# Retention attention and a two-layer feed-forward in one TensorE stream, token group by token group

## The chip, the cores and the metric

The kernel runs on one core of one Trainium2 chip. The metric is device time in microseconds (us) of one execution, median of several runs. A profile is one execution recorded by the hardware profiler; its span runs from the first to the last instruction.

Engines in the profile: PE is TensorE (matmuls), PEld its weight loads, DVE is VectorE, ACT is ScalarE, POOL is GpSimd (here it also issues the loads that convert to bf16), SP is SyncE. The kernel before has runs of about 303 to 307 us span and runs of about 310 to 311 us; the latter are marked slow. Ratios below use fast runs only.

## The reference, cut to what matters

```python
def _attn_ref(q, k, v):                       # q, k, v: (4, 8, 768, 64) float32
    gamma = 1.0 - 2.0 ** (-5.0 - np.arange(H))
    for t in range(S):
        state = gamma * state + outer(k[t], v[t])      # per batch and head: 64 x 64
        y[t] = (1 / sqrt(64)) * (q[t] @ state)

def _moe_ref(x, w_in, w_out, alpha):          # x: (3072, 512), 512 -> 2048 -> 512
    h = x @ w_in
    s = np.sin(alpha * h)
    g = h + s * s / (alpha + 1e-09)
    return g @ w_out
```

A chunked form of the attention works on 128 tokens at a time: within a chunk, a masked 128x128 score matrix; from earlier chunks, the state. There are 4 batches x 6 chunks = 24 chunks, 8 heads each.

## The kernel before

It has two stages, one after the other. Attention, per chunk index c and batch b (cuts marked `# ...`):

```python
for c in range(n_chunks):
    nc.gpsimd.dma_start(out=q_c, in_=dram_chunk(q, c))     # also k_c, v_c: 512 KB each
    nc.vector.tensor_mul(kw_c, k_c, wj_bc)                 # decay of k
    nc.scalar.copy(shat_bf[:64], shat_f32)                 # state to bf16
    for b in range(B):
        for h in range(H):                                 # q scaled and transposed
            nc.tensor.matmul(ptq[:64, h, :], q_c[:, b, h, :], Sgi[:, h, :], ...)
        nc.scalar.copy(qdT_gi, ptq[:64])
        # ... the same for k: 8 transposes, one ScalarE copy to kdT
        for h in range(H):                                 # scores, 64 rows of the array
            nc.tensor.matmul(psA[:, h, :], kdT[:, h, :], qdT_gi[:, h, :], ...)
        nc.vector.tensor_mul(aT, psA, mask01_bc)
        # ... psY: 8 matmuls with the state, 8 with v; ScalarE scales it into y_sbuf
        # ... psS: 8 matmuls k x v
        nc.vector.tensor_add(shat_f32[:, b], shat_f32[:, b], psS[:64])
    nc.vector.tensor_mul(shat_f32, shat_f32, gC_bc)        # decay of the state
```

Then the weights, and the feed-forward in 6 groups of 512 tokens:

```python
for g in range(n_groups):
    # ... 16 transposes of y_sbuf and 4 VectorE copies make xT (features on partitions)
    for ff in range(FF_SUB):                               # 16 steps
        for ks in range(K_SUB):                            # 4 matmuls of 512 columns
            nc.tensor.matmul(psH, w_in_bf[:, ks, ff, :], xT[:, ks, :], ...)
        nc.scalar.activation(out=s_sb, in_=psH, func=SIN, scale=alpha_sb[:, ff:ff + 1])
        nc.scalar.activation(out=s_sb, in_=s_sb, func=SQR, scale=rsq_alpha[:, ff:ff + 1])
        nc.vector.tensor_add(g_bf, psH, s_sb)
        for ts in range(n_tok_sub):                        # 4 matmuls of 512 columns
            nc.tensor.matmul(psO[ts], g_bf[:, ts * 128:(ts + 1) * 128], w_out_bf[:, ff, :], ...)
```

Of the kernel before, what the change touches and what calls it, by code (L numbers as in the profile page):

```python
# [9 lines left out]
F32 = mybir.dt.float32  # L10
BF16 = mybir.dt.bfloat16
EXP = mybir.ActivationFunctionType.Exp
SIN = mybir.ActivationFunctionType.Sin
SQR = mybir.ActivationFunctionType.Square
CPY = mybir.ActivationFunctionType.Copy
SQRT = mybir.ActivationFunctionType.Sqrt
# [3 lines left out]
def kernel(  # L20
# [13 lines left out]
    n_chunks = S // C  # L34
    BH = B * H
    NT = BH * n_chunks
    assert S % C == 0 and D == 64 and C == 128

    d_model = H * D
    d_ff = moe_w_in.shape[1]  # L40
    n_tok = B * S
    K_SUB = d_model // 128
    FF_SUB = d_ff // 128
    scale = 1.0 / math.sqrt(D)

    gammas = [1.0 - 2.0 ** (-5.0 - h) for h in range(H)]
# [3 lines left out]
    work = ctx.enter_context(tc.tile_pool(name="work", bufs=2))  # L50

    ident = consts.tile([128, 128], BF16, name="ident")
    make_identity(nc, ident)

    iota_free = consts.tile([128, 128], F32, name="iota_free")
    nc.gpsimd.iota(iota_free, pattern=[[1, 128]], channel_multiplier=0, base=0,
                   allow_small_or_imprecise_dtypes=True)
    iota_p = consts.tile([128, 1], F32, name="iota_p")
    nc.gpsimd.iota(iota_p, pattern=[[0, 1]], channel_multiplier=1, base=0,
                   allow_small_or_imprecise_dtypes=True)  # L60

    gi_free = consts.tile([128, H, 128], F32, name="gi_free")
    Sgi = consts.tile([128, H, 128], BF16, name="Sgi")
    wj_all = consts.tile([128, H], F32, name="wj_all")
    gC_all = consts.tile([128, H], F32, name="gC_all")
    for h in range(H):
        lng = math.log(gammas[h])
        nc.scalar.activation(out=gi_free[:, h, :], in_=iota_free, func=EXP, scale=lng)
        nc.vector.tensor_mul(Sgi[:, h, :], ident, gi_free[:, h, :])
        nc.scalar.activation(out=wj_all[:, h:h + 1], in_=iota_p, func=EXP, scale=-lng)  # L70
        nc.gpsimd.memset(gC_all[:, h:h + 1], gammas[h] ** C)
# [3 lines left out]
                            compare_op=mybir.AluOpType.is_ge, fill=0.0,  # L75
                            channel_multiplier=-1, base=0)
    mask01_bc = mask01[:, None, :].to_broadcast([128, H, 128])

    shat_f32 = big.tile([64, B, H, D], F32, name="shat_f32")
    nc.gpsimd.memset(shat_f32, 0.0)  # L80

    y_sbuf = big.tile([128, n_chunks, B, H, D], BF16, name="y_sbuf")

    gi_bc1 = gi_free[:64, :, :]
    gC_bc = gC_all[:64, None, :, None].to_broadcast([64, B, H, D])
    wj_bc = wj_all[:, None, :, None].to_broadcast([128, B, H, D])

    def dram_chunk(t, c):
        return t[:, :, c * C:(c + 1) * C, :].rearrange("b h s d -> s b h d")

    with tc.tile_pool(name="psum_r", bufs=1, space=bass.MemoryType.PSUM) as psr:
        for c in range(n_chunks):
            q_c = work.tile([128, B, H, D], BF16, name="q_c", tag="q_c", bufs=3)
            kw_c = work.tile([128, B, H, D], BF16, name="kw_c", tag="kw_c", bufs=3)
            v_c = work.tile([128, B, H, D], BF16, name="v_c", tag="v_c", bufs=3)
            k_c = work.tile([128, B, H, D], BF16, name="k_c", tag="k_c", bufs=3)
            nc.gpsimd.dma_start(out=q_c, in_=dram_chunk(q, c))  # L97
            nc.gpsimd.dma_start(out=k_c, in_=dram_chunk(k, c))  # L98
            nc.gpsimd.dma_start(out=v_c, in_=dram_chunk(v, c))  # L99
            nc.vector.tensor_mul(kw_c, k_c, wj_bc)  # L100

            shat_bf = work.tile([64, B, H, D], BF16, name="shat_bf", tag="sh")
            nc.scalar.copy(shat_bf[:64], shat_f32)  # L103

            for b in range(B):
                ptq = psr.tile([64, H, 128], F32, name="ptq", tag="qtg", bufs=1)
                for h in range(H):
                    nc.tensor.matmul(ptq[:64, h, :], q_c[:, b, h, :], Sgi[:, h, :],  # L108
                                     start=True, stop=True)
                qdT_gi = work.tile([64, H, C], BF16, name="qdT_gi", tag="qdT_gi")  # L110
                nc.scalar.copy(qdT_gi, ptq[:64])  # L111

                ptk = psr.tile([64, H, 128], BF16, name="ptk", tag="pt", bufs=2)
                for h in range(H):
                    nc.tensor.transpose(ptk[:64, h, :], kw_c[:, b, h, :], ident)  # L115
                kdT = work.tile([64, H, C], BF16, name="kdT", tag="kdT")
                nc.scalar.copy(kdT, ptk[:64])  # L117

                psA = psr.tile([128, H, 128], F32, name="psA", tag="psA", bufs=1)
                for h in range(H):  # L120
                    nc.tensor.matmul(psA[:, h, :], kdT[:, h, :], qdT_gi[:, h, :],  # L121
                                     start=(h % 4 == 0), stop=True, skip_group_check=True)
                aT = work.tile([128, H, 128], BF16, name="aT", tag="aT")
                nc.vector.tensor_mul(aT, psA, mask01_bc)  # L124

                psY = psr.tile([128, H, D], F32, name="psY", tag="psY", bufs=1)
                for h in range(H):
                    nc.tensor.matmul(psY[:, h, :], qdT_gi[:, h, :], shat_bf[:, b, h, :],  # L128
                                     start=(h == 0), stop=True, skip_group_check=True)
                for h in range(H):  # L130
                    nc.tensor.matmul(psY[:, h, :], aT[:, h, :], v_c[:, b, h, :],  # L131
                                     start=False, stop=True, skip_group_check=True)
                nc.scalar.mul(y_sbuf[:, c, b, :, :], psY, scale)  # L133

                psS = psr.tile([64, H, D], F32, name="psS", tag="psS", bufs=1)
                for h in range(H):
                    nc.tensor.matmul(psS[:64, h, :], kw_c[:, b, h, :], v_c[:, b, h, :],  # L137
                                     start=(h == 0), stop=True, skip_group_check=True)
                nc.vector.tensor_add(shat_f32[:, b, :, :], shat_f32[:, b, :, :], psS[:64])  # L139

            nc.vector.tensor_mul(shat_f32, shat_f32, gC_bc)  # L141

    w_in_bf = big.tile([128, K_SUB, FF_SUB, 128], BF16, name="w_in_bf")
    nc.gpsimd.dma_start(out=w_in_bf, in_=moe_w_in.rearrange("(ko ki) (fo fi) -> ki ko fo fi", ki=128, fi=128))

    w_out_bf = big.tile([128, FF_SUB, d_model], BF16, name="w_out_bf")
    nc.gpsimd.dma_start(out=w_out_bf, in_=moe_w_out.rearrange("(fo fi) n -> fi fo n", fi=128))

    alpha_sb = consts.tile([128, FF_SUB], F32, name="alpha_sb")
    for ff in range(FF_SUB):  # L150
        nc.sync.dma_start(out=alpha_sb[:, ff], in_=moe_alpha[ff * 128:(ff + 1) * 128])
    rsq_alpha = consts.tile([128, FF_SUB], F32, name="rsq_alpha")
    nc.gpsimd.tensor_scalar_add(rsq_alpha, alpha_sb, 1e-9)
    nc.scalar.activation(out=rsq_alpha, in_=rsq_alpha, func=SQRT)
    nc.vector.reciprocal(rsq_alpha, rsq_alpha)

    TOK_G = 512
    n_groups = n_tok // TOK_G
    n_tok_sub = TOK_G // 128

    out_view = out.rearrange("(t p) n -> p t n", p=128)

    with tc.tile_pool(name="psum_m", bufs=1, space=bass.MemoryType.PSUM) as psm:
        for g in range(n_groups):
            bc_list = [divmod(g * n_tok_sub + cc, n_chunks) for cc in range(n_tok_sub)]
            xT = work.tile([128, K_SUB, TOK_G], BF16, name="xT", tag="xT")
            for ks in range(K_SUB):
                pt = psm.tile([128, n_tok_sub, 128], BF16, name="ptxt", tag="psH", bufs=4)
                for cc in range(n_tok_sub):
                    b, c = bc_list[cc]  # L170
                    lhsT = y_sbuf[:, c, b, 2 * ks:2 * ks + 2, :].rearrange("p h e -> p (h e)")
                    nc.tensor.transpose(pt[:, cc, :], lhsT, ident)
                nc.vector.tensor_copy(xT[:, ks, :], pt.rearrange("p c s -> p (c s)"))  # L173

            psO = [psm.tile([128, d_model], F32, name=f"psO{ts}", tag=f"psO{ts}")
                   for ts in range(n_tok_sub)]
            for ff in range(FF_SUB):
                psH = psm.tile([128, TOK_G], F32, name="psH", tag="psH", bufs=4)
# [46 lines left out]
```

## Time and profile before

| | |
|---|---|
| median, all runs of the first series | 307.45 us (306.78 to 312.24, 4 runs) |
| profiled span (state slow by its clock, see below) | 310.9 us |
| wait for the first load | 0 to 13 us |
| attention | 13 to 114 us |
| feed-forward | 114 to 311 us, 31.0 us per full group |

First the profile page of the kernel before: the span in 40 equal slices, each digit a busy share in tenths, with the granted clock of TensorE and the GB/s that the loads moved.

```profile
span 310.9 us, 4916 instructions
...
PE   0189697969899977999899989998999899989991
...
PEclk9999979965955557999999999999999999999997
DMA  2999999999990000000300030003000300030003
GB/s 11 133 151 147 147 145 147 148 148 191 209 194 4 0 2 0 0 2 0 135 1 2 0 135 2 1 0 137 0 0 0 138 0 0 0 137 0 0 1 135
```

Loads fill the first 93 us. In the trace's clock records TensorE ran at half clock from 65 to 79 us and from 86 to 120 us. These records begin with the first change, at 24.2 us here. Before it the row reads 9 without a measurement: matmuls of 128 columns start 107 ns apart there, and 56 ns apart at full clock. How much of the attention runs at half clock differs from run to run: the profiled run has a mean clock of 0.912, like the runs marked slow (0.906 to 0.918), while the fast ones have 0.925 to 0.956.

Next, the busy time of each engine in one full group of the feed-forward, from one group's first output copy to the next group's (columns: the stretch, its length, busy us and count of each engine, then clock, DMA share, GB/s).

```profile
core 0: us, PE busy (x) PEld busy (x) DVE busy (x) ACT busy (x) POOL busy (x), PEclk, DMA share, GB/s
210.34:241.33 30.99, 29.64 (x142) 12.68 (x144) 14.62 (x24) 20.17 (x32) 0.00 (x0) 1.00 0.09 34
```

A group takes 31.0 us in this trace (five periods of 30.99 us), not the 32.0 us that the prediction and the expectation of e2 assume. TensorE looks 96% busy (29.64 of 30.99). That is not how full it is: a matmul's record (0.38 us for 512 columns) is longer than its distance to the next. Eight back to back take 1.90 us; their starts are 0.216 us apart, so the group's 128 matmuls need 27.6 us. The Trainium skill says this in "Trainium Kernel Development and Optimization", section "Performance Expectations": matmul busy time is a bad metric of distance to the peak. The trace agrees; the experiment e2 below takes 2.5 us out of such a "96% busy" group. With 0.9 us for the group's 16 transposes (56 ns each), 2.5 us of the 31.0 are waiting.

What the rest waits for is in the list of waits (engine and line, what it waited for, total us, times, longest):

```profile
DVE g_bf L186 <- ACT s_sb L184: 96.6, 66, 5.0
ACT s_sb L183 <- PE psH L180: 59.6, 23, 4.2
PEld L188 <- DVE g_bf L186: 30.4, 61, 1.9
PE psO L188 <- DVE g_bf L186: 5.2, 9, 1.4
```

The second layer's weight load (PEld L188: here g_bf is the stationary operand) waits for the sum that VectorE makes, which waits for sine and square on ScalarE.

### The profile page before, as it was taken

To read this page: it belongs to the slowest core of one execution; us is meant where nothing else is said; L and a number is where in the kernel's file an instruction comes from. 1 tells how busy PE (TensorE), PEld (TensorE's weight loads), DVE (VectorE), ACT (ScalarE), POOL (GpSimd) and SP (SyncE) were. 2 spreads that over 40 slices of the span, in tenths; PEclk is the share of its full clock that TensorE was granted. 3 is DMA by queue.
4 is the path that set the end of the run, shared out by engine and by line. 5 is a ranking of instruction groups with operands and counts; after the bars stand their busy time and mean duration, and the time that the engine had idled before them with its cause. 6 is when DMAs were issued, how large, how long until landed. Compare 5 with 4: busy or idle time off the path is not lost.

```text
span 310.9 us, 4916 instructions
## 1 busy us (share of the span) xinstructions
PE 264.5 (85%) x1999; PEld 150.8 (49%) x2016; DVE 160.5 (52%) x213; ACT 198.0 (64%) x290; POOL 35.9 (12%) x40
## 2 busy tenths in 40 slices
PE   0189697969899977999899989998999899989991
PEld 0177586758687763444443444444444444444430
DVE  2047879687756472434643464346434643463433
ACT  7147869765976626676567656765666566656660
POOL 9444444550000000000000000000000000000000
PEclk9999979965955557999999999999999999999997
DMA  2999999999990000000300030003000300030003
GB/s 11 133 151 147 147 145 147 148 148 191 209 194 4 0 2 0 0 2 0 135 1 2 0 135 2 1 0 137 0 0 0 138 0 0 0 137 0 0 1 135
DMA packets 82389, 20.23 MB, mean 65 GB/s; under 512 B 76736, under 2 KB 78784, under 8 KB 82368
## 3 DMA queue, kind: packets, MB, share of 16 engines
q0 software_dynamic: 76608, 13.63, 89.7%
q1 hardware_dynamic: 5760, 6.30, 5.9%
q8 instruction: 15, 0.25, 0.4%
q14 instruction: 6, 0.05, 0.1%
HBM read 27.27 MB, written 6.29 MB: 108 GB/s over the span
## 4 chain that ended last, share of the span: by engine, by line
PE 44%; ACT 16%; issue 13%; DVE 12%; POOL 8%; DMA 5%; ACTq 0%; POOLq 0%; DVEq 0%
PE psO L188 25%; PE psH L180 9%; ACT s_sb L183 8%; ACT s_sb L184 6%; DVE g_bf L186 5%; DMA k_c<-in_k_dram 3%; PE psA L121 3%; POOL q_c L97 3%; DVE o_sb L193 2%; POOL k_c L98 2%; POOL v_c L99 2%; DVE aT L124 2%; PE ptq L108 2%; PE ptk L115 2%; DVE shat_f L141 1%
## 5 line engine op out<-in xcount | busy, mean ns | idle before, releaser
L186 DVE TENSOR_TENSOR g_bf<-psH,s_sb 128x512 bf16<-128x512 f32 x96 | 63.9, 691 | 96.6 <-ACT s_sb L184 96.6
L183 ACT ACTIVATE s_sb<-psH,alpha_sb 128x512 f32<-128x512 f32 x96 | 62.3, 681 | 59.6 <-PE psH L180 59.6
L188 PE MATMUL psO<-w_out_bf,g_bf 128*128 128x512 bf16 x374 | 92.9, 381 | 7.6 <-DVE g_bf L186 5.2
L180 PE MATMUL psH<-xT,w_in_bf 128*128 128x512 bf16 x377 | 94.3, 384 | 2.1 <-DVE xT L173 1.4
L184 ACT ACTIVATE s_sb<-s_sb,rsq_alpha 128x512 f32<-128x512 f32 x96 | 65.8, 719 | 1.2
L188 PEld LDWEIGHTS <-g_bf 128*128 128x128 bf16 x384 | 32.2, 98 | 60.8 <-DVE g_bf L186 30.4
L180 PEld LDWEIGHTS <-w_in_bf 128*128 128x128 bf16 x384 | 37.8, 99 | 47.7 <-issue 5.4
L124 DVE TENSOR_TENSOR aT<-psA,mask 128x1024 bf16<-128x1024 f32 x24 | 29.3, 1219 | 18.2 <-PE psA L121 18.2
L111 ACT CAST qdT_gi<-ptq 64x1024 bf16<-64x1024 f32 x24 | 24.1, 1003 | 20.6 <-PE ptq L108 19.9
L108 PE MATMUL ptq<-Sgi,q_c 128*64 128x128 bf16 x192 | 21.6, 266 | 18.3 <-DMA q_c<-in_q_dram 13.0
L117 ACT COPY kdT<-ptk 64x1024 bf16<-64x1024 bf16 x24 | 24.0, 1005 | 8.2 <-PE ptk L115 4.5
L108 PEld LDWEIGHTS <-q_c 128*64 128x64 bf16 x192 | 16.4, 140 | 18.8 <-DMA q_c<-in_q_dram 13.0
L100 DVE TENSOR_TENSOR kw_c<-k_c,wj_all 128x2048 bf16<-128x2048 bf16 x6 | 13.7, 2287 | 14.8 <-DMA k_c<-in_k_dram 14.8
L115 PE MATMUL ptk<-ident,kw_c 128*64 128x128 bf16 x192 | 20.3, 263 | 1.0 <-ACT kdT L117 0.5
L121 PE MATMUL psA<-qdT_gi,kdT 64*128 64x128 bf16 x192 | 18.8, 254 | 2.7 <-DVE aT L124 2.0
L139 DVE TENSOR_TENSOR shat_f<-shat_f,psS 64x512 f32<-64x512 f32 x24 | 16.1, 673 | 7.2 <-PE psS L137 6.7
L193 DVE COPY o_sb<-psO 128x512 f32<-128x512 f32 x24 | 15.7, 689 | 7.5 <-DMA out_dram<-o_sb 4.6
L133 ACT ACTIVATE y_sbuf<-psY 128x512 bf16<-128x512 f32 x24 | 14.3, 595 | 7.5 <-PE psY L131 7.2
L115 PEld LDWEIGHTS <-kw_c 128*64 128x64 bf16 x192 | 16.5, 139 | 3.1 <-DVE kw_c L100 1.7
L121 PEld LDWEIGHTS <-kdT 64*128 64x128 bf16 x192 | 14.4, 111 | 4.6 <-issue 2.9
L128 PE MATMUL psY<-shat_bf,qdT_gi 64*128 64x64 bf16 x192 | 12.1, 214 | 4.0 <-ACT shat_bf L103 2.5
L137 PE MATMUL psS<-v_c,kw_c 128*64 128x64 bf16 x192 | 14.0, 223 | 0.4 <-DVE shat_f L139 0.4
(35 smaller groups left out, 138.9 us busy)
## 6 DMA issues: line engine op xcount, KB each, us to landing
out_dram<-o_sb SPq DMA_DIRECT2D x24, 256.0 KB, 2.1
q_c<-in_q_dram POOLq DMA_DIRECT2D x6, 512.0 KB, 10.6
k_c<-in_k_dram POOLq DMA_DIRECT2D x6, 512.0 KB, 10.5
v_c<-in_v_dram POOLq DMA_DIRECT2D x6, 512.0 KB, 10.6
w_in_bf<-in_moe_w_in_dram POOLq DMA_DIRECT2D x1, 2048.0 KB, 17.3
w_out_bf<-in_moe_w_out_dram POOLq DMA_DIRECT2D x1, 2048.0 KB, 26.6
alpha_sb<-in_moe_alpha_dram SPq DMA_DIRECT2D x16, 0.5 KB, 2.1
```

The lines of the kernel that those rows point to most:

```text
L108: nc.tensor.matmul(ptq[:64, h, :], q_c[:, b, h, :], Sgi[:, h, :], start=True, stop=True)
L111: nc.scalar.copy(qdT_gi, ptq[:64])
L115: nc.tensor.transpose(ptk[:64, h, :], kw_c[:, b, h, :], ident)
L117: nc.scalar.copy(kdT, ptk[:64])
L121: nc.tensor.matmul(psA[:, h, :], kdT[:, h, :], qdT_gi[:, h, :], start=(h % 4 == 0), stop=True, skip_group_check=True)
L124: nc.vector.tensor_mul(aT, psA, mask01_bc)
L180: nc.tensor.matmul(psH, w_in_bf[:, ks, ff, :], xT[:, ks, :], start=(ks == 0), stop=(ks == K_SUB - 1))
L183: nc.scalar.activation(out=s_sb, in_=psH, func=SIN, scale=alpha_sb[:, ff:ff + 1])
L184: nc.scalar.activation(out=s_sb, in_=s_sb, func=SQR, scale=rsq_alpha[:, ff:ff + 1])
L186: nc.vector.tensor_add(g_bf, psH, s_sb)
L188: nc.tensor.matmul(psO[ts], g_bf[:, ts * 128:(ts + 1) * 128], w_out_bf[:, ff, :], start=(ff == 0), stop=(ff == FF_SUB - 1))
L193: nc.vector.tensor_copy(o_sb, psO[ts])
```

## The change

Intent: keep TensorE fed all the time. While it runs the first layer of group g and the second layer of group g-1, it also runs, step by step, the attention of the chunks of group g+1. The new kernel walks the chunks in batch order (the six chunks of one batch in sequence), with groups of 2, 4, 4, 4, 4, 4, 2 chunks. The decay factors are put on q and k by one multiplication each, so that the state is a plain sum, which TensorE accumulates in one PSUM buffer (PSUM is the memory that the matmuls write to) over the six chunks of a batch. Two heads share one transpose (128 columns of features). The attention output comes out transposed, so it needs no transposes before the feed-forward.

The diff, cut to its core (the removed stages are those shown above):

```diff
+    groups = [2, 4, 4, 4, 4, 4, 2]
+    ctx.enter_context(tc.manual_schedule())
     ... constants: decay factors qg, kg by position and head; masks
+    def stage_scale(j, eng):                      # chunk j: q and k times their decay
+        eng.tensor_mul(qs, raw["q", j], qg[:, c, :, None].to_broadcast([128, H, D]))
+        eng.tensor_mul(ks, raw["k", j], kg[:, c, :, None].to_broadcast([128, H, D]))
+    def stage_T(j):                               # 8 transposes, one copy
+        for i, t in enumerate((st["qs", j], st["ks", j])):
+            for p in range(NP):
+                nc.tensor.transpose(pt[:, i * NP + p, :], t[:, 2 * p:2 * p + 2, :]..., ident)
+        nc.vector.tensor_copy(qkT, pt)
+    def stage_A(j):                               # scores: heads on array rows 0-63 and 64-127
+        for p in range(NP):
+            for e in range(2):
+                r = slice(64 * e, 64 * e + 64)
+                nc.tensor.matmul(pa[:, e, p, :], qkT[r, NP + p, :], qkT[r, p, :], ...)
+        nc.vector.tensor_mul(aT, pa, mask_bc)
+    def stage_Y(j):                               # output, transposed
+        if c > 0:
+            for p in range(NP):
+                nc.tensor.matmul(py[:, p, :], s_bd[c % 2][:, p, :], st["qkT", j][:, p, :], ...)
+        for p in range(NP):
+            for e in range(2):
+                nc.tensor.matmul(py[64 * e:64 * e + 64, p, :], raw["v", j][:, 2 * p + e, :],
+                                 st["aT", j][:, e, p, :], ...)
+        nc.scalar.copy(xT[g][:, :, o:o + C], py)
+    def stage_S(j):                               # state summed in PSUM
+        for p in range(NP):
+            nc.tensor.matmul(ps[:, p, :], ks pair p, v pair p, start=(c == 0 and p == 0), ...)
+        for e in range(2):
+            nc.scalar.copy(t[r, :, r], ps[r, :, r])
     ...
+    loads = w_in 0-3, chunks 2 3, w_out 0 1, chunks 4 5, w_out 2 3, chunks 6 ...
+    for fn in loads[:10]:                         # the rest: one per stage_T below
+        fn()
+    for j in range(groups[0]):
+        for fn in stages:
+            fn(j)
+    for g in range(NG + 1):
+        att = [(j, s) for the chunks j of group g+1, for s in range(4)]
+        for i in range(FF):                       # one step
+            ph = ff_in(g, i); s = ff_act(g, i, ph)         # 4 matmuls; sine, square
+            for j, sidx in att[na * i // FF:na * (i + 1) // FF]:
+                if sidx == 0:
+                    if loads: loads.pop(0)()
+                    stage_scale(j + 1, nc.vector if j + 1 < 6 else nc.gpsimd)
+                stages[sidx](j)
+            ff_add(g, i, ph, s)
+            ff_out(g - 1, i * n, n)               # n = 4 (2) second-layer matmuls
```

## The prediction

> **What bounds the kernel now.** Three stages, by the stretch table and the timeline of the trace (span 310.9 us).
>
> 1. 0 to 13 us: TensorE waits for the first q load.
> 2. 13 to 114 us: attention. The loads run at about 147 GB/s until 72 us; then the weights, 4.2 MB, until 93 us at about 205 GB/s. TensorE works in short bursts between copies; the granted clock falls to 0.5 between 64 and 116 us.
> 3. 114 to 311 us: feed-forward, 32.0 us per group of 512 tokens at clock 1.00. One layer step takes 2.0 us, though its 8 matmuls of 512 columns come 216 ns apart when back to back (8 in 1.90 us): 1.73 us. The rest is output transposes (57 ns each, 16 per group) and waits for the chain sine, square, add (0.69+0.72+0.69 us).
>
> The trace's 216 and 57 ns agree with the Trainium skill, "TensorE: Matmul & The Clock Gate", section "Back-to-back issue gap": N/2.4 GHz plus 2.5 ns.
>
> **What changes.** Per 128-token chunk TensorE now does 8 transposes, 8 score, 12 output and 4 state matmuls of 128 columns: 32 x 56 ns = 1.8 us, 41 us in all (estimate from the trace's spacing). The feed-forward stays 768 x 216 ns = 166 us. Sum: 207 us in one stream. Removed: 96 output transposes with VectorE copies (24 x 0.41 us), the state's additions, scalings and casts (16.1+13.7+11.4 us); weights load early.
>
> Per step in the steady groups: TensorE 0.86+0.45+0.86 = 2.2 us; ScalarE 1.35 + a quarter of (0.6 + two state copies of about 0.4) = 1.7 us; VectorE 0.69 + a quarter of (0.7+1.22+0.69) = 1.35 us. TensorE binds, and the sine-square-add latency (2.1 us) fits inside two steps. GpSimd scales q and k from chunk 6 on: the skill's "GPSIMD Engine Reference", section 3.1, gives 4497 ns for 2048 elements of a two-input operation; no trace here has it; my estimate is 1.3 us for 512. With three load issues of about 0.9 us (fitted to 0.76, 1.17, 1.68 us for 512, 2048, 4096 packets) that is 5.3 us per chunk, under the chunk's 7 to 9 us.
>
> **Sum (estimates).** First two chunks, serially at a cold clock: 22 us. Group 0 is paced by loads (w_in, chunks 2 to 5, w_out: about 150 to 205 GB/s) and ScalarE: ends near 47 us. Group 1 (TensorE and ScalarE both about 1.8 us per step): 30. Groups 2 to 4: 36 each, 108. Group 5: 32. Group 6 (256 tokens): 21.5. Last output matmuls 7, last copy and store 3.5. Span 249; times are about 3 us below the profiled span: **246 us**, range 236 to 262. Chances: faster by over 2% 0.97, within 2% 0.02, slower 0.01.
>
> **What would show it.** Granted clock 1.0 from about 45 us on, no 0.5 stretch after; TensorE steps of about 2.2 us with little idle; ScalarE near 75 to 80% busy there; no added activation table loads (copies run under the sine table); before that, waits named for loads, scalings, copies.
>
> **What would make it wrong.** GpSimd multiplications much slower than 1.3 us, so that scaling paces the chunks; the in-order TensorE queue stalling at attention stages behind VectorE or ScalarE; small matmuls costing more than 56 ns between the large ones; table reloads between copy and sine (1.28 us each); the start, where loads and serial stages could cost 10 us more or less.

## The result and the profile after

The new kernel took 248.03 us (247.86 to 248.22, 4 runs), the kernel before 307.45 us. The ratio of fast runs is 0.8083, with a 95% interval of 0.8033 to 0.8133. (A ratio is the mean time of one kernel's fast runs over that of the other's in the same rounds, so it is not quite the ratio of the two medians.)

The profile page of the new kernel, same rows as before:

```profile
span 246.4 us, 4059 instructions
...
PE   0146748799999999999999999999999999999993
...
PEclk9999986999999999999999999999999999999999
DMA  9999999999998879849957965901101110012112
GB/s 53 117 205 177 193 164 194 118 95 78 88 133 55 92 85 67 87 66 72 99 67 85 64 80 73 80 26 45 43 0 47 43 43 22 23 43 85 45 43 85
```

From the ninth slice on (49 us), TensorE is at 9 up to the last slice and the clock is at 9. The loads are now spread over the first 160 us.

The same trace in stretches cut at the starts of the groups (0 to 21.69: the first two chunks, where the clock of 1.00 is not measured, as said above; then groups 0, 1, 2 to 4, 5, 6; the last second layer; the last store):

```profile
0.00:21.69 21.69, 6.33 (x60) 4.41 (x61) 7.11 (x20) 5.11 (x10) 16.62 (x28) 1.00 1.26 136
21.69:51.03 29.34, 20.69 (x188) 14.68 (x188) 18.27 (x31) 20.44 (x44) 19.66 (x23) 0.88 1.85 163
51.03:79.89 28.86, 28.27 (x221) 14.22 (x222) 18.04 (x25) 25.80 (x43) 25.88 (x28) 1.00 1.25 88
79.89:183.40 103.51, 103.51 (x754) 52.11 (x753) 60.89 (x84) 80.05 (x130) 46.30 (x49) 1.00 0.65 67
183.40:214.19 30.79, 30.79 (x188) 14.80 (x187) 16.72 (x24) 24.36 (x38) 0.00 (x0) 1.00 0.10 35
214.19:235.42 21.23, 21.14 (x130) 12.62 (x129) 9.35 (x20) 16.17 (x34) 0.00 (x0) 1.00 0.13 50
235.42:242.35 6.93, 6.90 (x32) 2.94 (x30) 1.72 (x3) 0.18 (x1) 0.00 (x0) 1.00 0.20 76
242.35:246.40 4.05, 0.00 (x0) 0.00 (x0) 0.69 (x1) 0.00 (x0) 0.00 (x0) 1.00 0.17 65
```

In groups 2 to 4 TensorE has no gap (103.51 of 103.51 us); ScalarE is busy 80.05 us, 77%. Three groups take 34.5 us each and include 12 chunks of attention. The kernel before took 31.0 us for such a group without any attention.

The timeline of TensorE over some three steps in group 2 (start, length, line, what, count):

```profile
97.90 0.39 PE L134 MATMUL pt<-ident,qs 128*128 128x128 bf16 x4
98.12 0.39 PE L134 MATMUL pt<-ident,ks 128*128 128x128 bf16 x4
98.34 1.03 PE L218 MATMUL po<-w_out,gT 128*128 128x512 bf16 x4
99.21 1.03 PE L195 MATMUL ph<-xT,w_in 128*128 128x512 bf16 x4
100.17 0.40 PE L145 MATMUL pa<-qkT 64*128 64x128 bf16 x8
100.50 1.04 PE L218 MATMUL po<-w_out,gT 128*128 128x512 bf16 x4
101.37 1.03 PE L195 MATMUL ph<-xT,w_in 128*128 128x512 bf16 x4
102.33 0.41 PE L163 MATMUL py<-aT,vr 128*64 128x128 bf16 x8
102.67 1.04 PE L218 MATMUL po<-w_out,gT 128*128 128x512 bf16 x4
103.55 1.03 PE L195 MATMUL ph<-xT,w_in 128*128 128x512 bf16 x4
104.41 0.39 PE L176 MATMUL ps<-vr,ks 128*128 128x128 bf16 x4
```

From one ph to the next is one step: 2.16 us at 99.21, 2.18 us at 101.37. An attention stage fills 0.2 to 0.66 us between the two layers and none of these lines has a wait behind it.

### The profile page after: what moved, and what is told of

It reads as the page before. It is cut to its first block, busy times and chain, and to the rows that moved or that the text cites. A ratio compares the mean times of both kernels' runs of the same rounds, so it can differ in the third digit from the quotient of the medians.

```text
span 246.4 us, 4059 instructions
## 1 busy us (share of the span) xinstructions
PE 217.6 (88%) x1568; PEld 115.8 (47%) x1568; DVE 132.8 (54%) x208; ACT 172.1 (70%) x294; POOL 108.5 (44%) x127
## 4 chain that ended last, share of the span: by engine, by line
PE 72%; DMA 12%; ACT 5%; POOL 5%; issue 2%; DVE 2%; POOLq 0%
PE po L218 33%; PE ph L195 29%; DMA w_out<-in_moe_w_out_dram 5%; DMA w_in<-in_moe_w_in_dram 4%; DMA vr<-in_v_dram 3%; PE pt L134 3%; PE py L163 3%; ACT s L202 3%; PE pa L145 2%; ACT s L203 2%; PE py L159 1%; POOL qr L66 1%; PE ps L176 1%; POOL kr L66 1%; DVE gT L207 1%
## 5 line engine op out<-in xcount | busy, mean ns | idle before, releaser
L207 DVE TENSOR_TENSOR gT<-ph,s 128x512 bf16<-128x512 f32 (+1 forms) x112 | 68.7, 613 | 83.5 <-ACT s L203 83.5
L195 PE MATMUL ph<-xT,w_in 128*128 128x512 bf16 (+1 forms) x448 | 104.6, 358 | 2.1 <-DVE gT L207 1.8
L202 ACT ACTIVATE s<-ph,alpha_sb 128x512 f32<-128x512 f32 (+1 forms) x112 | 70.0, 625 | 42.9 <-PE ph L195 30.8
L218 PE MATMUL po<-w_out,gT 128*128 128x512 bf16 x384 | 98.9, 380 | 0.0
L203 ACT ACTIVATE s<-s,rsq_alpha 128x512 f32<-128x512 f32 (+1 forms) x112 | 74.0, 661 | 3.6
L195 PEld LDWEIGHTS <-w_in 128*128 128x128 bf16 x448 | 44.3, 101 | 47.4 <-issue 4.4
L218 PEld LDWEIGHTS <-gT 128*128 128x128 bf16 x384 | 33.2, 98 | 29.1
L148 DVE TENSOR_TENSOR aT<-pa,mask 128x1024 bf16<-128x1024 f32 x24 | 29.3, 1221 | 4.6 <-PE pa L145 4.6
L66 POOL DMA_DIRECT2D qr<-in_q_dram x24 | 22.5, 938 | 1.3 <-POOLq L280 0.8
L66 POOL DMA_DIRECT2D vr<-in_v_dram x24 | 21.7, 905 | 0.8 <-DMA w_in<-in_moe_w_in_dram 0.8
L66 POOL DMA_DIRECT2D kr<-in_k_dram x24 | 21.6, 899 | 0.0
L222 DVE COPY o_sb<-po 128x512 f32<-128x512 f32 x24 | 16.4, 681 | 5.0 <-PE po L218 5.0
L136 DVE COPY qkT<-pt 128x1024 bf16<-128x1024 bf16 x24 | 16.4, 682 | 2.5 <-PE pt L134 2.4
```

The lines of the kernel that those rows point to most:

```text
L66: nc.gpsimd.dma_start(out=t, in_=src[b, :, c * C:(c + 1) * C, :].rearrange("h s d -> s h d"))
L148: nc.vector.tensor_mul(aT.rearrange("p e n t -> p (e n) t"), pa.rearrange("p e n t -> p (e n) t"), mask_bc)
L195: nc.tensor.matmul(ph, w_in[:, i, f * 128:(f + 1) * 128], xT[g][:, i, :], start=(i == 0), stop=(i == KS - 1))
L202: nc.scalar.activation(out=s, in_=ph, func=ACTF.Sin, scale=alpha_sb[:, f:f + 1])
L203: nc.scalar.activation(out=s, in_=s, func=ACTF.Square, scale=rsq_alpha[:, f:f + 1])
L207: nc.vector.tensor_add(gT[g][:, f, :], ph, s)
```

## The experiments

Two questions were open after this. Where do the 59 us come from: running the attention inside the feed-forward, a leaner attention, or a feed-forward that no longer waits within its step? And what bounds the new kernel, in the middle and in its first 51 us? Below, fast runs of the variants are compared with the new kernel's 248.03 us; unedited on another chip it took 247.99 us (e0_again), so the choice of chip matters little.

### e1_seq: the new attention first, then the new feed-forward

```diff
     stage_scale(0, nc.vector); stage_scale(1, nc.vector)
     ... chunks 0 and 1 as before
+    for j in range(groups[0], NJ):
+        if loads: loads.pop(0)()
+        ... stage_scale(j + 1, nc.vector)
+        for fn in stages: fn(j)
     for g in range(NG + 1):
-        att = [(j, s) for the chunks of group g+1 ...]
+        att = []
```

> The new kernel with the attention of all 24 chunks run before the first feed-forward group (its scalings on VectorE, so that GpSimd only issues loads), everything else kept. Theory O (the gain comes mostly from running the attention inside the feed-forward): attention takes about 4 to 5 us per chunk when its stages run serially, the feed-forward about 170 to 180 us, so about 280 us (268 to 295). Rival L (the gain comes mostly from the leaner attention and the feed-forward that no longer waits within a step): at most 262 us.

Measured: 332.64 us (2 runs, ratio 1.0878 to before). It is slower than the kernel before, and slower than the range given. One chunk takes 5.03 us, as the timeline of TensorE shows:

```profile
99.67 0.58 PE L134 MATMUL pt<-ident,qs 128*128 128x128 bf16 x4
100.05 0.63 PE L134 MATMUL pt<-ident,ks 128*128 128x128 bf16 x4
101.47 0.61 PE L145 MATMUL pa<-qkT 64*128 64x128 bf16 x8 [0.79 <-DVE qkT L136]
102.01 0.61 PE L159 MATMUL py<-qkT,s_bd 128*128 128x128 bf16 x4
103.39 0.64 PE L163 MATMUL py<-aT,vr 128*64 128x128 bf16 x8 [0.78 <-DVE aT L148]
```

Every stage waits for the copy of the one before, because nothing stands between them. The transposes also run at half speed: 4 take 0.58 to 0.63 us here and 0.39 us in the new kernel, and their single starts are 107 ns apart here and 56 ns there. The feed-forward behind it took from 138.6 to 331.4 us, 193 us, not the 170 to 180 us assumed. Its first group (256 tokens, no second layer to run beside it) took 21.5 us of that, from 139.2 to 160.8 us: matmuls of 256 columns were still 213 ns apart (109 ns in the new kernel), and every two steps (2.58 us) TensorE waited 0.66 us for VectorE's sum.

### e12_seq_skew: the same, with the chunks' stages skewed

```diff
-        for fn in stages: fn(j)
+        stage_T(j)
+        if j - 1 >= groups[0]: stage_A(j - 1)
+        if j - 2 >= groups[0]: stage_Y(j - 2); stage_S(j - 2)
```

(with a few more buffers, and py in the PSUM buffers of ph.)

> As e1_seq (attention of all chunks before the feed-forward, which took 332.6 us, 5.03 us per chunk), but with the stages of neighbouring chunks skewed: transposes of chunk j, scores of j-1, output and state of j-2. If e1_seq was slow only because one chunk's stages ran as a chain with nothing between them, a chunk falls to what VectorE needs (0.68+1.22+2x0.69 = 3.3 us) or a half-clock TensorE (about 3.6 us): 24 x 1.4 us less, about 300 us (292 to 308), near the kernel before. If instead loads (2.65 us per chunk) or something else held it: 320 us or more.

Measured: 295.79 us (2 runs, ratio to before 0.9623, 0.9567 to 0.9678), inside the forecast. A chunk now takes 2.93 us and VectorE is the limit, busy in 25.00 of 25.00 us:

```profile
60.00:85.00 25.00, 16.44 (x264) 12.42 (x261) 25.00 (x35) 10.29 (x25) 24.66 (x29) 1.00 2.43 155
```

So the leaner attention together with the reordered feed-forward, but one after the other, is worth 4% over the kernel before. The remaining 48 us (295.8 to 248.0) are the difference to running them at the same time. That is a difference between two builds, not the least that overlap is worth: e12 has all scalings on VectorE, its limit, and its first feed-forward group ran at half clock (102 to 126 us in its trace). A leaner build of the two stages one after the other was not tried.

### e2_before_ffpipe: the kernel before, only its feed-forward reordered

```diff
-            for ts in range(n_tok_sub):
-                nc.tensor.matmul(psO[ts], g_bf[:, ...], w_out_bf[:, ff, :], ...)
+            # second layer of group g-1, 4 matmuls per step; gT of a whole group kept
+            nc.tensor.matmul(po[0], gT[g - 1][:, f, ts * 128:(ts + 1) * 128], w_out_bf[:, f, :], ...)
+            # the transposes of group g+1 at steps 2, 6, 10, 14
```

> The kernel before with its attention untouched, only the feed-forward reordered: second-layer matmuls lag one group of 512 tokens behind the first layer's, output transposes of the next group within the steps. If the 0.27 us per step that TensorE lost there was waiting for the sine-square-add chain, a full group falls from 32.0 to about 28.6 us (1.73 us per step plus transposes), with one ScalarE-paced group of 22 us at the start and 14 us of second layer at the end: about 294 us (290 to 298). If the order did not matter: 303 us or more.

Measured: two runs of 301.43 us (fast, span 299.7) and 309.2 us (slow); beside fast runs of before of 304.7 to 307.3 us. One fast run gives no interval, so the total is told as 3 to 6 us less, unconfirmed. The mechanism is plain in the profile of the fast run: a full group fell from 31.0 to 28.5 us, which is the 27.6 us of matmuls and 0.9 us of transposes; the 2.5 us of waiting are gone (0.16 us per step, not the 0.27 us that the expectation has from a group of 32.0 us).

```profile
165.00:193.50 28.50, 28.34 (x142) 13.40 (x144) 14.78 (x24) 22.52 (x33) 0.00 (x0) 1.00 0.10 38
```

The total fell short of the expected 294 us because the pipeline has to be filled and drained: the first group, which has no second layer beside it, took from 108.8 to 140.0 us, 31.2 us (3.2 us of transposes, then 1.75 us per step, with TensorE waiting 0.93 and 0.31 us in turn for VectorE's sum) instead of the 22 us put down, and the last second layer with its copies and stores 18.0 us instead of 14. The whole feed-forward took 191 us against 196.6 us before. Ordering the feed-forward better is thus a small part of the gain by itself.

### e3_no_square: less ScalarE work and less latency

```diff
-        nc.scalar.activation(out=s, in_=s, func=ACTF.Square, scale=rsq_alpha[:, f:f + 1])
```

> The new kernel without the square on ScalarE (a wrong result on purpose): 0.72 us less on ScalarE per step and 0.72 us less latency from first-layer matmul to add. Theory T (TensorE's 2.17 us per step is the limit in groups 1 to 6): only group 0 and a little of group 1 shrink, 244 to 247 us. Rival A (ScalarE's pace or the sine-square-add latency limits): 238 us or less.

Measured: 245.18 us, 2 runs; the result is wrong. Taking away half of the feed-forward's ScalarE work changes 3 us, all of it in the first two groups. From VectorE's first sum of group 2 to that of group 5 (48 steps) the new kernel, e3 and e4 below took, in this order:

```profile
83.00:185.92 102.92, 102.92 (x747) 51.76 (x747) 60.30 (x84) 79.49 (x128) 44.58 (x48) 1.00 0.63 66
79.37:182.38 103.01, 101.74 (x733) 51.62 (x745) 60.49 (x84) 44.90 (x80) 45.59 (x49) 1.00 0.63 66
80.60:167.75 87.15, 82.43 (x646) 43.57 (x656) 59.20 (x83) 77.92 (x129) 44.15 (x47) 1.00 0.74 78
```

The stretch is as long without the square (102.92 and 103.01 us), with ScalarE busy 44.90 instead of 79.49 us. ScalarE and the latency of the chain do not bind in the middle.

### e4_half_k: less TensorE work

```diff
-        for i in range(KS):
+        for i in range(KS // 2):
             nc.tensor.matmul(ph, w_in[:, i, ...], xT[g][:, i, :], ...)
```

> The new kernel with only 2 of the 4 first-layer matmuls (a wrong result on purpose): 0.43 us less TensorE work per full step. Theory T: groups 2 to 4 fall from 2.17 us per step to the next limit, ScalarE at about 1.74 us; group 5 from 1.95 to about 1.55, group 6 by 0.2 per step, group 1 stays ScalarE-bound: about 29 us less, 219 us (214 to 225). Rival A: 238 us or more.

Measured: 221.23 us, 2 runs; wrong result. 27 us less. A step in the middle fell from 2.17 to 1.80 us (19 steps from 81.65 to 115.93 us), not by the full 0.43 us. What takes up the rest was not settled: ScalarE was busy 89% of the stretch above (77.92 of 87.15 us, 1.62 us per step), and TensorE now waits at times for the copy after the transposes (0.2 us before the scores at 87.75 us). Group 5 fell from 30.3 to 24.8 us. Together with e3 this shows that TensorE binds in groups 2 to 5.

### e5_e_outer: the order of matmuls on the two halves of the array

```diff
-        for p in range(NP):
-            for e in range(2):
+        for e in range(2):
+            for p in range(NP):
```

(in stage_A and in the v part of stage_Y.)

> The new kernel with the two loops over head pairs and heads exchanged in the score and output stages, so that neighbouring matmuls use the same 64 rows (or columns) of the array instead of alternating. Theory C (alternating halves run side by side: 8 in 0.40 us, but entering and leaving such a stage costs about 0.2 us): each such stage grows by about 0.22 us, 0.45 us per chunk, over the 18 chunks in TensorE-bound groups 8 us: 256 us (253 to 259). Rival N (a matmul of 128 columns costs 56 ns wherever its rows lie, so 8 cost 0.45 us either way): 248 us within 1%.

Measured: 248.35 us (248.17 to 248.57, 4 runs), no change, as rival N forecast. But its reason, 56 ns for each matmul wherever its rows lie, does not fit the trace. In the new kernel's stage_A the single matmul starts come in pairs: 100.167 and 100.171, 100.234 and 100.237, 100.290 and 100.293, 100.346 and 100.349 us (starts of single records in the trace). In e5, whose program has four matmuls of the one half and then four of the other, the starts also come in pairs, 13 ns apart and 56 ns from pair to pair (100.432 and 100.445, 100.487 and 100.501). In the kernel before, where all heads used the same 64 rows, eight starts are 56 ns apart one by one. So in the new kernel the two halves run side by side, and exchanging the loops did not undo it. Why not stays open: the records name neither the half nor the place in the program, so whether the matmuls of e5 were put in another order before the chip or on it cannot be seen. Theory C was therefore not tested. The timeline of e5 has the same length of the stage as the new kernel's:

```profile
100.36 0.41 PE L145 MATMUL pa<-qkT 64*128 64x128 bf16 x8
...
102.54 0.42 PE L163 MATMUL py<-aT,vr 128*64 128x128 bf16 x8
```

What eats the gain of the pairs is the border. The 512-column matmul before stage_A starts at 99.856 us, so at 216 ns the next could start at 100.072; it starts at 100.167, 95 ns late. From the last pair (100.349) to the next 512-column matmul (100.497) are 148 ns instead of 56, 92 ns late. Stage_A thus fills 0.425 us, against 0.45 us for eight matmuls at 56 ns. The stages of full 128x128 matmuls (transposes, state) have no such gaps: from the last transpose to the next matmul are 56 ns. The Trainium skill, "TensorEngine Tiling (Array Packing)", section "Key Properties", says that changing the tiling mode drains TensorE, without a figure; the gaps of 92 to 95 ns, only at the borders of half-array stages, fit this, but no run here changed the mode alone.

### e6_state_sbuf and e7_y_plain: two parts of the change undone

```diff
# e6_state_sbuf
-            nc.tensor.matmul(ps[:, p, :], ..., start=(c == 0 and p == 0), ...)
+            nc.tensor.matmul(ps[:, p, :], ..., start=(p == 0), ...)
+        nc.vector.tensor_add(sh, sh, ps)           # copy for c == 0
-            nc.scalar.copy(t[r, :, r], ps[r, :, r])
+            nc.scalar.copy(t[r, :, r], sh[r, :, r])
# e7_y_plain
-                nc.tensor.matmul(py[64 * e:64 * e + 64, p, :], raw["v", j][...], st["aT", j][:, e, p, :], ...)
+                nc.tensor.matmul(py[:, p, 64 * e:64 * e + 64], st["aT", j][:, e, p, :], raw["v", j][...], ...)
+        nc.scalar.copy(y, py)                      # then a fifth stage:
+            nc.tensor.transpose(px[:, p, :], st["y", j][:, p, :], ident)
+        nc.vector.tensor_copy(xT[g][:, :, o:o + C], px)
```

They ran with the unedited new kernel as a yardstick on the same chip.

> The new kernel unedited, on the same chip as the three that follow, as their yardstick: 248 us (247.5 to 248.5).

> The new kernel with one part undone: the state is kept in on-chip memory and VectorE adds each chunk's k-v product to it (0.69 us per chunk), instead of being summed by TensorE in one bank. Theory T (TensorE's stream is the limit, VectorE is under 60% busy there, and the next chunk's output needs the state only 3 steps later): 248 us within 0.5%. Rival (the state's path is on the chain of waits, so summing it in PSUM is part of the gain): 251 us or more.

> The new kernel with another part undone: attention output made with tokens on the partitions, copied by ScalarE, transposed by 4 TensorE matmuls in a fifth stage and copied by VectorE. TensorE: output stage 4 x 56 + 8 x about 30 ns instead of 0.66 us, plus 0.22 us of transposes: about the same 0.68 us; VectorE 0.41 us more per chunk. Theory T: 248 us within 1%. Rival (the transposed output saves TensorE work or a wait): 252 us or more.

Measured: yardstick 247.99 us (247.93 to 248.17), e6 248.17 us (247.96 to 248.50), e7 248.88 us (248.79 to 249.22), 4 runs each. The sum in PSUM is worth nothing measurable here and the transposed output 0.9 us. Both parts of the change remove VectorE work, and VectorE is not the limit: it was busy 60.89 of 103.51 us in the middle. Undoing the transposed output also leaves TensorE's work nearly as it was, because the 64-column matmuls with v are shorter than the 128-column ones. In a kernel whose attention stands alone (e12, VectorE full) the same removals could count; that was not run.

### e9_load_order, e10_load_order2, e11_start: the first 51 us

In the new kernel group 0 takes 29.3 us, though its TensorE work and its ScalarE work are about 21 us each. TensorE's longest waits there are for the copy after the transposes (2.88 us at 36.0 us). VectorE runs in order, and ahead of that copy stands the scaling of the next chunk, which waits for its load (the first line is VectorE's scaling, the second TensorE's scores):

```profile
33.81 0.69 DVE L126 TENSOR_TENSOR qs<-qr,qg 128x512 bf16<-128x512 bf16 x1 [1.34 <-DMA qr<-in_q_dram]
36.00 0.61 PE L145 MATMUL pa<-qkT 64*128 64x128 bf16 x8 [2.88 <-DVE qkT L136]
```

The loads come as w_in, chunks 2 3, half of w_out, chunks 4 5, though w_out is first needed in group 1.

```diff
# e9
-    loads = w_in 0-3, chunks 2 3, w_out 0 1, chunks 4 5, w_out 2 3, chunks 6 ...    (10 at the start)
+    at the start: w_in 0, chunk 2, w_in 1, chunk 3, w_in 2, chunk 4, w_in 3, chunk 5,
+                  chunk 6, w_out 0, 1, 2, chunk 7, w_out 3;   then one per stage_T: chunk 8, 9, ...
# e10, against e9
+    at the start: ... chunk 6, w_out 0, 1;   then one per stage_T: w_out 2, w_out 3, chunk 7, nothing, chunk 8, ...
# e11 = e10 and
+    the identity, mask and position constants before the first loads on GpSimd
+    stages T0 T1 A0 A1 Y0 S0 Y1 S1 instead of T0 A0 Y0 S0 T1 A1 Y1 S1
```

> The new kernel with only the order of the loads changed: pieces of w_in and chunks 2 to 5 alternate, then chunk 6, then w_out and chunk 7, all issued at the start. Theory W (the first 51 us are paced by loads that arrive in the wrong order): group 0 falls from 29 to about 21 us: 239 us (236 to 243). Rival S (group 0 is paced by its own chain of ScalarE and VectorE work): 246 us or more.

Measured: 253.15 us (252.46 to 253.68, 4 runs), slower by 5 us. Group 0's own steps did get quicker (21.7 to about 45.5 us), but then TensorE stood:

```profile
PEld L134 <- POOL qs L126: 8.2, 1, 8.2
PE pt L134 <- POOL qs L126: 7.7, 1, 7.7
POOL qr L66 <- DMA w_out<-in_moe_w_out_dram: 1.6, 1, 1.6
```

The transposes of chunk 6 waited 7.7 us for the scaling of chunk 6 on GpSimd. The edit had put the loads of chunks 8 to 11 ahead of that scaling in GpSimd's queue. Each of the 12 issues keeps GpSimd busy about 0.9 us, and the program has eight completion semaphores for GpSimd's loads, so the ninth issue waits for the first load to land (the last line shows such a wait, for w_out). After its wait TensorE also ran at half clock from 50 to 60 us.

> e9_load_order repaired. There group 0 fell from 29.3 to 24.7 us, but GpSimd, which runs in order and keeps at most eight loads in flight, had the loads of chunks 8 to 11 ahead of the scaling of chunk 6, so TensorE then waited 7.7 us for it. Here those loads come after that scaling. Theory W: the 4.6 us of group 0 are kept and the wait goes: 243.5 us (241.5 to 245.5). If a wait for chunk 6 stays, about 248 us.

Measured: 245.18 us (243.55 to 245.54, 4 runs). With those loads moved behind the scaling, the wait is gone and group 1 starts at about 48.0 instead of 51.0 us. TensorE ran at half clock from about 38 to 45 us in this profile, so not all of e9's quicker group 0 came through.

> e10_load_order2 with an earlier start: the constants that the scalings need are made on GpSimd before the first loads are issued, and the stages of chunks 0 and 1 alternate instead of running one chunk after the other. The first transposes move from 11.0 to about 8.5 us and the first feed-forward matmul from 21.7 to about 17 us; all later stages move with it unless the loads of chunks 4 to 6 then hold group 0: 240 us (237.5 to 243).

Measured: 240.65 us (239.41 to 241.78, 4 runs; ratio to the kernel before 0.7873, 0.7823 to 0.7923), against 247.99 us for the new kernel on the same chip: 3.0% less. The first transposes start at 6.65 us (new kernel: 11.01), the first feed-forward matmul at 19.1 us (21.7), group 1 at about 42.7 us (51.0). The first transposes came earlier than forecast (8.5), the first feed-forward matmul later (17). The page shows TensorE at 9 from the seventh slice (36 us) on:

```profile
span 238.1 us, 4057 instructions
...
PE   0267666999999999999999999999999999999993
```

This is the fastest version, and its result is correct.

## Why the prediction was right

The forecast was 246 us with a range of 236 to 262; 248.03 us were measured. Point by point:

| term | forecast, us | measured, us |
|---|---|---|
| first two chunks | 22 | 21.7 |
| group 0 | 25 (ends near 47) | 29.3 (ends at 51.0) |
| group 1 | 30 | 28.9 |
| groups 2 to 4 | 108 | 103.5 |
| group 5 | 32 | 30.8 |
| group 6 | 21.5 | 21.2 |
| last second layer, copy, store | 7 + 3.5 | 6.9 + 4.05 |
| span | 249 | 246.4 |

1. *TensorE binds, at about 2.2 us per step.* Right: 2.16 us (34.5 us per group of 16), no gap, clock 1.00. e3 and e4 confirm it: less ScalarE work changes 3 us, less TensorE work 27 us.
2. *ScalarE 75 to 80% busy there.* Right: 77%. No added table loads: there are three of 1283 ns, as before.
3. *The size of the attention on TensorE, 32 matmuls x 56 ns.* The sum was right (about 1.76 us against 1.8 us for a chunk with state), the way to it was not: half-array matmuls start in pairs, and the borders of their stages cost about 0.19 us each time. The two deviations cancel, which is luck. The spacing formula that the prediction cites is given in its section for an isolated matmul; for a stream of weight loads and matmuls the same section has about 81 ns (128 columns) and 131 ns (512 columns), where these traces show 56 and 216 ns.
4. *GpSimd.* A multiplication of 512 elements took 1.05 us, not 1.3 us, and a load issue 0.90 to 0.94 us. Scaling did not pace the chunks in the new kernel; e9 shows that it can, once loads stand ahead of it.
5. *The start.* The forecast named loads, scalings and copies as what TensorE would wait for; that is what the list of waits has. Group 0 was 4 us too short in the sum. Most of the missing term is the order: the forecast counted bytes, and did not see that an in-order VectorE puts the wait for the next chunk's load ahead of the current chunk's copy. e10, which changes the order of the loads alone, wins 3 us; e11, with an earlier start besides, 7 us.
6. *"Times are about 3 us below the profiled span"* was wrong. It came from comparing one profiled run in the slow state with a median of mostly fast runs. A timed run is about 1.7 us above its own span. This error of 4.7 us and a sum of stages 2.6 us too long partly cancelled, again by luck.
7. *The kernel before.* The forecast's 32.0 us per group and 2.0 us per step are 31.0 and 1.94 us in its own trace. No term of its sum was built on them.
8. *What was removed.* The forecast listed the removed transposes and state operations without saying what they are worth. e6 and e7 say it: nothing, and 0.9 us. Most of the gain is the overlap: attention and feed-forward one after the other take 295.8 us even with well-ordered stages (e12), 332.6 us with the stages in the order of the new kernel (e1), and 248.0 us interleaved.

Open: the total of e2 rests on one fast run; how much of the old attention's time was due to the half clock was not separated; the earlier loading of the weights was not tested apart; and why TensorE's clock in group 0 falls in some runs and not in others was not settled.

## What to carry to other kernels

When two stages of a kernel leave gaps on the same engine, put the steps of the one into the gaps of the other before making either leaner: here that was worth 48 us (e12 against the new kernel), while two of the removals inside the attention were worth 0.9 us or less. Then price the merged stream by matmul spacing, not by busy time, and check per step that every other engine and the longest latency fit under it. In-order queues need the same care as the arithmetic: what stands ahead of an operation in its engine's queue, a load issue or a scaling for the next chunk, can cost more than the operation itself.

## What the Trainium skill lacked or had wrong

- "TensorE: Matmul & The Clock Gate", section "Part 3: Packing small matmuls", has matmuls start strictly in program order. Whether that holds here is open. In e5 four matmuls of one array half stand before four of the other in the program, and the starts in the trace are pairs 13 ns apart with 56 ns from pair to pair. Four of the same half in sequence would be 56 ns apart each, as in the kernel before. The records name neither the half nor the place in the program, so a change of order before the chip would look the same.
- "TensorEngine Tiling (Array Packing)", section "Key Properties", gives no figure for the drain at a change of mode. Here entering a half-array stage cost 95 ns and leaving it 92 ns (no run shows that the drain is the cause); pairing eight 128-column matmuls saves about 4 x 56 = 224 ns.
- "DMA: Bandwidth & Descriptors", section "Anatomy of one DMA — SWDGE (gpsimd) path", calls descriptor generation small and gives no figure for it. Here 72 load issues kept GpSimd busy for 65.8 us (22.5+21.7+21.6), about 0.9 us for an issue of 1024 packets, in the queue that also computes. What part of an issue is descriptor generation the trace does not say.
- "TensorE: Matmul & The Clock Gate", section "Part 1: The HAM clock gate (the "warmup" mystery)", ties the clock to how busy TensorE has been, without a share of busy time. In e1 the attention kept it busy 70.4 of 120 us (59%) and its matmuls stayed at 107 ns; in e12, at 16.4 of 25 us (66%), they ran at 56 ns. These are not a threshold: the same attention of e12 ran at half clock from 88.4 to 95.3 us. The same page, under "Seeing it yourself", warns that the clock's trace events are unreliable: e1's clock reads 1.00 throughout the half-speed attention (mean 0.997), since its record begins only at the first change.
